# SSD scan and feed-forward: decay matrices as running products on VectorE, the scan in pairs of chunks, scores in four row tiles, weight conversion shared with ScalarE

## The chip, the cores and the metric

One core of one Trainium2 chip runs the kernel. The metric is device time in microseconds (us) of one execution; before the change it is 528.14 us, the median of 3 runs (527.07 to 530.32).

## The reference

A gated linear scan over 4 batches, 8 heads, 768 tokens, head dimension 32 and state size 16 (`x` is [4, 8, 768, 32], `a` [4, 8, 768], `B` and `C` [4, 8, 768, 16]), and then a feed-forward on the 3072 tokens of width 256:

```python
log_a = log(clip(a, 1e-6, 1))
# per chunk, state carried on:
cum = cumsum(la);  L = exp(cum_i - cum_j) where i >= j
y = (C B^T * L) x  +  (C state) * exp(cum)
state = exp(sum(la)) * state + sum_j B_j x_j exp(cum_last - cum_j)
# then, tokens x (head, dim) = 3072 x 256:
h = x @ w_in                     # 256 x 2048
out = (h * sigmoid(1.702 h)) @ w_out   # 2048 x 256
```

The weights arrive as float64 and are rounded to float32 on the chip. All else is float32.

## The kernel before

**Tiling.** The scan runs in chunks of 128 tokens, all 8 heads of a batch together: 24 chunks `n`, 6 per batch. Four chunks make a group of 512 tokens, 6 groups `g`. In a group the feed-forward is `hidden` (16 blocks `f` of 128 features, two 128x128 by 128x512 products each, SiLU on ScalarE, L329 to L335) and then `project` (4 blocks of 128 tokens, 16 products of 256 columns each, L337 to L345). A float32 product shows in the trace as two matmul instructions.

**One chunk of the scan.** `log_decay` (L226, GpSimd) writes log a above the diagonal, `decay` (L234) sums it with two 512-column products (`seg`, L239) and takes Exp on ScalarE (L242), and `causal` (L244, GpSimd) clears the other half: that is the decay matrix `L`, [j, head, i], 128x1024. `scale` (L250, GpSimd) decays B to the chunk's end and C from its start. `turn` (L261) transposes B, C and scaled C on TensorE and copies them out on VectorE. `scores` (L277) makes C.B for four heads at a time in two row tiles of 64 (`cb`, L284), and VectorE multiplies it into `L` (L285). `advance` (L288) makes the next state (`A` L296, VectorE L299 and L301). `finish` (L306) makes `y` from the old state (L315) and from `L` (L320, four column tiles of 32); VectorE copies it to `yT` (L326).

**Weights.** `narrow(i)` (L124 to L157) turns one of 16 pieces of 512 KB of float64 bits into float32: five instructions on VectorE and two on ScalarE. Pieces 0 to 7 are `w_in`, 8 to 15 `w_out`; a piece serves two blocks `f`. `fetch` (L111) loads a piece, five ahead.

**Order.** Every engine runs its instructions in the order in which they are written (`in_order`, L24). First come 8 steps (L349 to L363), each with a decay and a `narrow`; the first four also scan a chunk of group 0. Then, for each group (L365 to L396): 16 blocks of `hidden`, with the other 8 `narrow` in group 0 and, between the blocks, the scan of the next group's four chunks (one step of a chunk behind each block); then 4 blocks of `project`, each preceded by one decay matrix of the group after the next. All DMAs, loads and stores, are issued on SP's queue in written order (L101, L122, L162, L345). PSUM has two buffers each for `h` and `o` (`ff`), for `seg` and `cb` (`big`), and for the small tiles (`sm`).

Of the kernel before, what the change touches and what calls it, by code (L numbers as in the profile page):

```python
# [6 lines left out]
    make_identity,  # L7
    make_lower_triangular,
    make_upper_triangular,
)  # L10
# [9 lines left out]
P = 128  # L20
TG = 512


def in_order(tc):  # L24
    """Each engine runs its instructions in the order in which they are written."""
    last = {}
    for ins in list(tc.nc.cur_bb.bb.instructions):
        before = last.get(ins.engine)
        if before is not None:
            tc.add_manual_dep(  # L30
                ins, before.name,
                mybir.DependencyInfo(mybir.DependencyClass.NoSync,
                                     mybir.DependencyReason.DATA),
                reason="in_order")
        last[ins.engine] = ins
# [3 lines left out]
def kernel(  # L39
# [22 lines left out]
    nc = tc.nc  # L62

    # float64 weights, in two words an element
# [13 lines left out]
    assert NF // CG == 4 and NH * N == P and NH * D == DM and HB * D == P and HB * P == TG  # L78
# [6 lines left out]
    ps = ctx.enter_context(tc.tile_pool(name="ps", bufs=2, space=bass.MemoryType.PSUM))  # L85

    # ---- loads
    a_sb = const.tile([BH, S], FP32, name="a_sb")
# [4 lines left out]
    def load(g):  # L93
        rx[g] = raw.tile([P, CG, NH, D], FP32, tag="x", name=f"x{g}")
        rb[g] = raw.tile([P, CG, NH, N], FP32, tag="b", name=f"b{g}")
        rc[g] = raw.tile([P, CG, NH, N], FP32, tag="c", name=f"c{g}")
        for k in range(CG):
            b, c = divmod(g * CG + k, NC)
            sl = slice(c * P, (c + 1) * P)
            for dst, src in ((rb, B), (rc, C), (rx, x)):  # L100
                nc.sync.dma_start(out=dst[g][:, k], in_=src[b, :, sl, :].rearrange("h s d -> s h d"))  # L101

    # ---- weights: float64 bits, [low word, high word], to float32, a piece at a time
    PF = 2
    AHEAD = 5
# [18 lines left out]
    def narrow(i):  # L124
        """w = (-1)^sign x 2^(E - 1023) x (1 + high 2^-20 + low 2^-52), with the power of two
        0 below float32's normal range and infinite above it"""
# [4 lines left out]
        # an eighth of the mantissa: (1 + high 2^-23) - 7/8 is exact, the sum with low rounds  # L131
        u = wide.tile([P, PN], U32, tag="u", name=f"u{i}")
        nc.vector.tensor_scalar(out=u, in0=hi, scalar1=0x000FFFFF, scalar2=0x3F800000,
                                op0=ALU.bitwise_and, op1=ALU.bitwise_or)
        e = wide.tile([P, PN], U32, tag="e", name=f"e{i}")
        nc.vector.tensor_scalar(out=e, in0=hi, scalar1=0x7FF00000, scalar2=None,
                                op0=ALU.bitwise_and)
        m = wide.tile([P, PN], FP32, tag="m", name=f"m{i}")
        nc.scalar.activation(m, lo, AF.Copy, scale=2.0 ** -55)
        # the exponent field, moved to float32's place and bias; multiples of 2^20 are exact  # L140
        z = wide.tile([P, PN], FP32, tag="z", name=f"z{i}")
        nc.scalar.activation(z, e, AF.Relu, scale=8.0, bias=bias[:, 0:1])  # L142
        p2 = wide.tile([P, PN], U32, tag="p2", name=f"p2{i}")
        nc.vector.tensor_scalar(out=p2, in0=z, scalar1=float(255 << 23), scalar2=None,  # L144
                                op0=ALU.min)
        nc.vector.scalar_tensor_tensor(out=m, in0=u.bitcast(FP32), scalar=-0.875, in1=m,  # L146
# [5 lines left out]
        else:  # L152
            dst, split = w_out[:, f:f + PF, :], PF
        nc.vector.scalar_tensor_tensor(  # L154
            out=dst, in0=m.rearrange("p (k e) -> p k e", k=split), scalar=8.0,
            in1=p2.bitcast(FP32).rearrange("p (k e) -> p k e", k=split),
            op0=ALU.mult, op1=ALU.mult)  # L157

    bias = const.tile([P, 1], FP32, name="bias")
    nc.vector.memset(bias, -float(896 << 23))  # L160

    nc.sync.dma_start(out=a_sb, in_=a.rearrange("b h s -> (b h) s"))  # L162
    load(0)
    for i in range(AHEAD):
        fetch(i)

    # ---- constants
    ident = const.tile([P, P], FP32, name="ident")
    make_identity(nc, ident)
    upper = const.tile([P, P], FP32, name="upper")  # L170
    make_upper_triangular(nc, upper, 1.0, diag=True)
    lower = const.tile([P, P], FP32, name="lower")
    make_lower_triangular(nc, lower, 1.0, diag=False)
    ones = const.tile([P, P], FP32, name="ones")
    nc.vector.memset(ones, 1.0)
# [3 lines left out]
    nc.vector.memset(same, 1.0)  # L179
# [6 lines left out]
    # rows (head, state): one in the column head mod HB  # L186
    part = const.tile([P, HB], FP32, name="part")
    nc.vector.tensor_tensor(out=part, in0=same[:, 0:HB, 0], in1=same[:, HB:NH, 0], op=ALU.add)

    # ---- log a, and every decay that one token, or a whole chunk, has to itself  # L190
    a_ps = ps.tile([P, NC, BH], FP32, tag="sm", name="a_ps")
    for c in range(NC):
        nc.tensor.transpose(out=a_ps[:, c], in_=a_sb[:, c * P:(c + 1) * P],
                            identity=ident[0:BH, 0:BH])
    la = const.tile([P, NC, BH], FP32, name="la")
    nc.vector.tensor_scalar(out=la, in0=a_ps, scalar1=1e-6, scalar2=1.0,
                            op0=ALU.max, op1=ALU.min)
    nc.scalar.activation(la, la, AF.Ln)  # L198

    def summed(lhsT, name):  # L200
        t = ps.tile([P, NC, BH], FP32, tag="sm", name=name)
        nc.tensor.matmul(out=t, lhsT=lhsT, rhs=la, start=True, stop=True)
        return t

    to_end = const.tile([P, NC, BH], FP32, name="to_end")
    nc.scalar.activation(to_end, summed(lower, "end_ps"), AF.Exp)
    from_start = const.tile([P, NC, BH], FP32, name="from_start")
    nc.scalar.activation(from_start, summed(upper, "start_ps"), AF.Exp)
    whole_h = const.tile([P, NC * NB, NH], FP32, name="whole_h")
    nc.vector.tensor_tensor(  # L210
        out=whole_h, in0=summed(ones, "whole_ps").rearrange("p c (b h) -> p (c b) h", h=NH),
        in1=same[:, :, 0].unsqueeze(1).to_broadcast([P, NC * NB, NH]), op=ALU.mult)
    whole = const.tile([P, NC * NB], FP32, name="whole")
    nc.vector.tensor_reduce(out=whole, in_=whole_h, op=ALU.add, axis=AX.X)
    nc.scalar.activation(whole, whole, AF.Exp)

    # ---- the scan, a chunk at a time
    st = {}
# [3 lines left out]
    def heads(t, n):  # L222
        b, c = divmod(n, NC)
        return t[:, c, b * NH:(b + 1) * NH]

    def log_decay(n):  # L226
        """log a of token k where k <= i: [k, head, i]"""
        st[n] = {}
        st[n]["lu"] = lu = ssd.tile([P, NH, P], FP32, tag="lu", name=f"lu{n}")
        nc.gpsimd.tensor_tensor(  # L230
            out=lu, in0=upper.unsqueeze(1).to_broadcast([P, NH, P]),
            in1=heads(la, n).unsqueeze(2).to_broadcast([P, NH, P]), op=ALU.mult)

    def decay(n):  # L234
        """the decay from j to i, [j, head, i]; nothing for i < j yet"""
        lu = st[n].pop("lu")
        seg = ps.tile([P, 2, HB, P], FP32, tag="big", name=f"seg{n}")
        for t in range(2):
            nc.tensor.matmul(out=seg[:, t], lhsT=lower, rhs=lu[:, t * HB:(t + 1) * HB],  # L239
                             start=True, stop=True)  # L240
        st[n]["L"] = L = ssd.tile([P, NH, P], FP32, tag="L", name=f"L{n}", bufs=CG + 1)
        nc.scalar.activation(L, seg.rearrange("p t h i -> p (t h) i"), AF.Exp)  # L242

# [44 lines left out]
    def advance(n):  # L288
# [4 lines left out]
        if c == NC - 1:  # L293
            return
# [134 lines left out]
```

## Time and profile before

| | |
|---|---|
| runs | 530.32, 528.14, 527.07 us; median 528.14 |
| profiled execution | span 525.5 us from first to last instruction; its time with what lies around the span is not listed. The median is 2.6 us above the span |
| TensorE busy | 473.9 us (90%) |
| VectorE, ScalarE, GpSimd busy | 158.4, 116.9, 96.9 us |
| chain that ended last | TensorE 82%, VectorE 11%, ScalarE 2% |
| mean granted TensorE clock | 0.955 of full speed |

The profile is of one execution. A share of busy time is a mean over stages: here a stage of some 91 us before the first `h`, group 0 until 172 us, and then five groups that look alike.

### The profile page before, as it was taken

How to read it: one execution, taken by the hardware profiler on the slowest of the kernel's cores; microseconds unless marked ns; L12 is line 12 of the kernel's file. 1: busy time of each engine (PE TensorE's matmuls, PEld its weight loads, DVE VectorE, ACT ScalarE, POOL GpSimd, SP SyncE). 2: the span in 40 equal slices, each digit the busy share in tenths (PEclk: the TensorE clock that was granted, in tenths of full speed). 3: DMA queues.
4: the chain of work that ended last, by engine and by line, in shares of the span. 5: the costliest groups of instructions: out<-in, count | busy, mean ns of one | idle time of the engine just before them, and what ended most of it. 6: DMA issues, size and time to landing. Idle time of an engine off the chain costs nothing.

```text
span 525.5 us, 4898 instructions
## 1 busy us (share of the span) xinstructions
PE 473.9 (90%) x1932; PEld 284.7 (54%) x1932; DVE 158.4 (30%) x283; ACT 116.9 (22%) x167; POOL 96.9 (18%) x108
## 2 busy tenths in 40 slices
PE   4544476879999999999999999999999999999997
PEld 2222132333678444687444786445875446864586
DVE  1556567887600343000353001322002331000000
ACT  3111124434411122210323102223012221013200
POOL 6033344120222030231030312300321000000000
PEclk9677777989999999999999999999999999999999
DMA  8611254810000700000700002400000000000000
GB/s 118 249 40 41 50 71 131 153 37 1 1 20 11 90 0 2 1 20 19 82 0 1 10 11 46 54 1 1 11 20 11 0 0 1 22 20 0 1 20 20
DMA packets 82758, 18.23 MB, mean 35 GB/s; under 512 B 75536, under 2 KB 78608, under 8 KB 82736
## 3 DMA queue, kind: packets, MB, share of 16 engines
q1 hardware_dynamic: 82736, 17.93, 17.1%
q8 instruction: 15, 0.25, 0.2%
q14 instruction: 7, 0.06, 0.0%
HBM read 14.78 MB, written 3.15 MB: 34 GB/s over the span
## 4 chain that ended last, share of the span: by engine, by line
PE 82%; DVE 11%; ACT 2%; SPq 2%; issue 1%; DMA 1%; ACTq 0%; DVEq 0%
PE o L340 32%; PE h L332 29%; PE seg L239 7%; PE cb L284 5%; PE y L320 3%; DVE p L148 3%; PE y L315 3%; PE A L296 2%; DVE m L146 2%; ACT z L142 2%; SPq L101 2%; DVE p L144 1%; DVE w_in L154 1%; PE tp L266 1%; DMA bits<-in_moe_w_in_dram 1%
## 5 line engine op out<-in xcount | busy, mean ns | idle before, releaser
L332 PE MATMUL h<-yT,w_in 128*128 128x512 f32 x384 | 184.1, 610 | 0.0
L340 PE MATMUL o<-w_out,gT 128*128 128x256 f32 x768 | 168.8, 379 | 0.0
L340 PEld LDWEIGHTS o<-w_out,gT 128*128 128x128 f32 x768 | 145.8, 190 | 27.2 <-issue 8.3
L332 PEld LDWEIGHTS h<-yT,w_in 128*128 128x128 f32 x384 | 69.7, 193 | 76.7 <-issue 60.5
L335 ACT ACTIVATE gT<-h 128x512 f32<-128x512 f32 x96 | 57.3, 597 | 183.6 <-PE h L332 183.5
L343 DVE TENSOR_SCALAR ob<-o 128x256 f32<-128x256 f32 x24 | 10.2, 425 | 208.2 <-PE o L340 208.2
L246 POOL TENSOR_SCALAR_AFFINE_SELECT L<-L 128x1024 f32<-128x1024 f32 x24 | 27.5, 1146 | 232.0 <-ACT L L242 232.0
L242 ACT ACTIVATE L<-seg 128x1024 f32<-128x1024 f32 x24 | 24.6, 1023 | 144.4 <-PE seg L239 144.4
L239 PE MATMUL seg<-lu,lower 128*128 128x512 f32 x96 | 50.0, 647 | 3.2 <-POOL lu L230 3.2
L284 PE MATMUL cb<-CT,BT 64*128 64x512 f32 x96 | 30.9, 723 | 23.5 <-DVE CT L271 23.5
L230 POOL TENSOR_TENSOR lu<-upper,la 128x1024 f32<-128x1024 f32 x24 | 47.6, 1993 | 1.6 <-ACT la L198 1.6
L285 DVE TENSOR_TENSOR L<-L,cb 128x1024 f32<-128x1024 f32 x24 | 29.3, 1220 | 36.8 <-PE cb L284 36.8
L239 PEld LDWEIGHTS seg<-lu,lower 128*128 128x128 f32 x96 | 18.7, 205 | 21.5 <-issue 15.3
L284 PEld LDWEIGHTS cb<-CT,BT 64*128 64x128 f32 x96 | 8.2, 205 | 40.3 <-issue 15.3
L320 PE MATMUL y<-L,x 128*32 128x128 f32 x384 | 21.0, 301 | 3.1 <-DVE L L285 3.1
L315 PEld LDWEIGHTS y<-CsT,S 128*128 128x128 f32 x80 | 15.0, 208 | 13.0 <-issue 12.5
L326 DVE COPY yT<-y 128x256 f32<-128x256 f32 x24 | 10.2, 423 | 39.3 <-PE y L320 39.3
L257 POOL TENSOR_TENSOR Cs<-c,from_start 128x128 f32<-128x128 f32 x24 | 10.3, 430 | 56.7 <-PE tp L266 56.7
L266 PE MATMUL tp<-ident,Cs 128*128 128x128 f32 x24 | 6.8, 284 | 14.5 <-POOL Cs L257 14.5
L315 PE MATMUL y<-CsT,S 128*128 128x128 f32 x80 | 19.0, 323 | 0.0
L148 DVE SCALAR_TENSOR_TENSOR p<-bits,p 128x512 uint32<-128x512 uint32 x16 | 17.7, 1108 | 0.0
L144 DVE TENSOR_SCALAR p<-z 128x512 uint32<-128x512 f32 x16 | 9.1, 570 | 24.2 <-ACT z L142 24.2
(56 smaller groups left out, 204.1 us busy)
## 6 DMA issues: line engine op xcount, KB each, us to landing
bits<-in_moe_w_in_dram SPq DMA_DIRECT2D x8, 512.0 KB, 5.5
bits<-in_moe_w_out_dram SPq DMA_DIRECT2D x8, 512.0 KB, 3.5
x<-in_x_dram SPq DMA_DIRECT2D x24, 128.0 KB, 3.8
out_dram<-ob SPq DMA_DIRECT2D x24, 128.0 KB, 1.7
b<-in_B_dram SPq DMA_DIRECT2D x24, 64.0 KB, 3.7
c<-in_C_dram SPq DMA_DIRECT2D x24, 64.0 KB, 3.6
a_sb<-in_a_dram SPq DMA_DIRECT2D x1, 96.0 KB, 2.3
```

The source lines that it names most:

```text
L148: nc.vector.scalar_tensor_tensor(out=p2, in0=hi, scalar=0x80000000, in1=p2, op0=ALU.bitwise_and, op1=ALU.bitwise_or)
L230: nc.gpsimd.tensor_tensor(out=lu, in0=upper.unsqueeze(1).to_broadcast([P, NH, P]), in1=heads(la, n).unsqueeze(2).to_broadcast([P, NH, P]), ...
L239: nc.tensor.matmul(out=seg[:, t], lhsT=lower, rhs=lu[:, t * HB:(t + 1) * HB], start=True, stop=True)
L242: nc.scalar.activation(L, seg.rearrange("p t h i -> p (t h) i"), AF.Exp)
L246: nc.gpsimd.affine_select(out=L, in_=L, pattern=[[0, NH], [1, P]], compare_op=ALU.is_ge, fill=0.0, base=0, channel_multiplier=-1)
L284: nc.tensor.matmul(out=cb[:, t], lhsT=BT[r], rhs=CT[r], start=True, stop=True)
L285: nc.vector.tensor_tensor(out=L, in0=L, in1=cb.rearrange("p t h i -> p (t h) i"), op=ALU.mult)
L315: nc.tensor.matmul(out=y[:, t], lhsT=state[n - 1][:, t * HB:(t + 1) * HB], rhs=s["CsT"], start=True, stop=False, skip_group_check=True)
L320: nc.tensor.matmul(out=y[D * q:D * q + D, t], lhsT=rx[g][:, k, h], rhs=s["L"][:, h], start=(c == 0), stop=True, tile_position=(0, D * q), ...
L332: nc.tensor.matmul(out=h, lhsT=w_in[:, k, f * P:(f + 1) * P], rhs=yT[g][:, k], start=(k == 0), stop=(k == NK - 1))
L335: nc.scalar.activation(gT, h, AF.Silu, scale=GELU_SCALE)
L340: nc.tensor.matmul(out=o, lhsT=gT[f][:, k * P:(k + 1) * P], rhs=w_out[:, f], start=(f == 0), stop=(f == NF - 1))
```

## The change

- **Decay matrices.** `a` itself, broadcast to all 128 partitions, is loaded per chunk by a DMA (`spread`, 512 KB on arrival): for the first group from the input, with clipping on VectorE; later from a clipped copy with zeros at chunk starts, which the kernel writes to DRAM (`scratch`). One `tensor_tensor_scan` per chunk, 1024 elements, gives `L`: state = a x state + identity. `seg`, its Exp, `log_decay`, `causal` and `scale` are gone. `Be` takes its factor from the last column of `L`, on VectorE. The decay from the chunk's start comes from a scan per batch over rows of `a` (`decay_rows`), and is applied to C behind its transpose.
- **Pairs.** A step of the scan now takes two chunks (`p`, 12 pairs), two pairs per group. `scores` uses four row tiles of 32, each with its own PSUM bank (`cb`, one buffer of four banks).
- **Evacuation.** Copies of transposed B and C and of `y` move from VectorE to ScalarE.
- **Conversion.** In a piece the minimum moves to ScalarE: three instructions there (z, p2, m, one behind the other), five on VectorE. Fetches run four ahead instead of five.
- **Order.** Before the first `h` there are now 4 decays, 2 pairs and 3 pieces (before: 8 decays, 4 chunks, 8 pieces); 9 pieces and 4 decays lie between the blocks of `hidden` of group 0, 4 pieces, 4 decays and 2 pairs in its `project`, which runs over `f` outside and tokens inside. Pairs of later groups lie in `hidden`, decays in `project`.

```diff
+    def spread(n):
+        ra[n] = raw.tile([P, NH * P], FP32, tag="a", name=f"a{n}", bufs=4)
+        src = a[b, :, c * P:(c + 1) * P] if n < CG else scratch[b, c]
+        nc.sync.dma_start(out=ra[n]..., in_=src.unsqueeze(0).to_broadcast([P, NH, P]))
...
+    a_sb load; spread(0); load(0); spread(1); spread_rows(0); fetch(0); load(1)
+    spread(2); spread(3); fetch(1..3)
...
     def narrow(i):
+        nc.vector.tensor_scalar(out=e, in0=hi, 0x7FF00000, bitwise_and)
+        nc.scalar.activation(z, e, AF.Relu, scale=-8.0, bias=edge[:, 0:1])
+        nc.scalar.activation(p2, z, AF.Relu, scale=-1.0, bias=edge[:, 1:2])
+        nc.scalar.activation(m, lo, AF.Copy, scale=2.0 ** -52)
+        nc.vector.tensor_scalar(out=u, in0=hi, 0x000FFFFF, 0x41000000, and, or)
+        nc.vector.scalar_tensor_tensor(out=m, in0=u, scalar=-7.0, in1=m, add, add)
         nc.vector.scalar_tensor_tensor(out=p2, in0=hi, 0x80000000, in1=p2, and, or)
+        nc.vector.tensor_tensor(out=dst, in0=m, in1=p2, op=ALU.mult)
...
     def decay(n):
+        if n < CG:
+            nc.vector.tensor_scalar(out=t, in0=t, max 1e-6, min 1.0)
+            nc.vector.memset(first element of each head, 0.0)
+        nc.vector.tensor_tensor_scan(out=Ls[p][:, k], data0=t, data1=idents,
+                                     initial=0.0, op0=ALU.mult, op1=ALU.add)
+        if k == 1:
+            nc.vector.tensor_tensor(out=BE[p], in0=rb[p], in1=last column of Ls[p], mult)
...
+    def decay_rows(b):   # clip, memset, copy on GpSimd, then on VectorE:
+        nc.vector.tensor_tensor_scan(out=since[b], data0=t, data1=first, ...)
...
     def turn(p):
+        4 transposes (B, C of both chunks) into tp
+        nc.scalar.activation(s["BT"], tp[:, 0], AF.Copy)
+        for q in range(Q):   # 2
+            nc.scalar.activation(s["CT"][:, :, q], tp[:, 1], AF.Copy, scale=part[:, q:q + 1])
+        nc.vector.tensor_tensor(out=s["CsT"], in0=tp[:, 1], in1=since[b], op=ALU.mult)
...
     def scores(p):
+        cb = ps.tile([P, R, 2, Q * P], FP32, tag="cb", name=f"cb{p}", bufs=1)
+        for k in range(2):
+            for r in range(R):   # 4
+                nc.tensor.matmul(out=cb[:, r, k], lhsT=BT[rows, k], rhs=CT[rows, k],
+                                 tile_position=(32 * r, 0), ...)
+        nc.vector.tensor_tensor(out=Lv, in0=Lv, in1=cb, op=ALU.mult)   # 2048 elements
...
     def finish(p):   # all state products, then all products with L, then:
+        nc.scalar.activation(yT[g][...], y, AF.Copy)
...
+    def project_all(g, gT, between):   # group 0
+        for f in range(NF):
+            for do in between.get(f, []): do()
+            for k in range(CG):
+                nc.tensor.matmul(out=o[k // 2][:, k % 2], lhsT=gT[f][...], rhs=w_out[:, f], ...)
+        for k in range(CG): store(g, k, ...)
...
+    decay(0); decay(1); decay_rows(0); narrow(0)
+    for p in range(PG):   # 2
+        turn(p); advance(p); scores(p)
+        if p + 1 < PG: decay(2 * p + 2); decay(2 * p + 3)
+        narrow(1 + p); finish(p)
+    spread_rows(1); load(2); load(3); spread(4..7)
...
+    # hidden of group 0, after block f: narrow(3..7) at 0..4,
+    # decay(4..7) at 5, 7, 9, 11, narrow(8..11) at 6, 8, 10, 12
+    # project of group 0, before f: narrow(12..15) at 0, 2, 4, 6, decay(8..11) at 3, 7, 11, 15,
+    # pairs 2 and 3: turn, advance, scores, finish at 0, 1, 3, 6 and 8, 9, 11, 14; decay_rows(1) at 5
+    # hidden of groups 1 to 4: pairs at 0, 1, 2, 6 and 8, 9, 10, 14; project: one decay per block
```

## Rows read from the trace of the kernel before

**Rows 1.** Busy time in stretches of the span: us, engines, granted clock, DMA share, GB/s

```profile
0.00:91.00 91.00, 48.29 (x165) 22.07 (x166) 49.47 (x78) 21.36 (x30) 34.82 (x41) 0.77 0.43 100
91.00:172.10 81.10, 75.32 (x311) 45.27 (x310) 42.18 (x80) 27.73 (x40) 15.61 (x16) 0.96 0.18 37
172.10:247.90 75.80, 75.80 (x323) 46.30 (x323) 16.99 (x30) 14.94 (x21) 15.05 (x16) 1.00 0.15 21
467.30:525.50 58.20, 55.08 (x192) 36.11 (x191) 2.12 (x5) 9.55 (x16) 0.00 (x0) 1.00 0.03 12
```

**Rows 2.** Chain of waits in order of time: start us, us, what

```profile
222.02 1.72 PE seg L239 x4
...
439.46 27.82 PE o L340 x128
467.28 27.47 PE h L332 x64
```

**Rows 3.** Timeline of TensorE around one chunk: start us, us, engine, line, operation

```profile
171.93 1.88 PE L332 MATMUL h<-yT,w_in 128*128 128x512 f32 x4
...
173.65 0.27 PE L266 MATMUL tp<-ident,b 128*128 128x128 f32 x1
...
173.97 1.88 PE L332 MATMUL h<-yT,w_in 128*128 128x512 f32 x4
...
175.78 1.13 PE L284 MATMUL cb<-CT,BT 64*128 64x512 f32 x4
...
176.84 1.98 PE L332 MATMUL h<-yT,w_in 128*128 128x512 f32 x4
...
180.81 0.38 PE L315 MATMUL y<-CsT,S 128*128 128x128 f32 x2
...
182.26 1.98 PE L332 MATMUL h<-yT,w_in 128*128 128x512 f32 x4
```

**Rows 4.** Timeline of VectorE over one piece of weights, first and last instruction

```profile
94.68 0.42 DVE L133 TENSOR_SCALAR u<-bits 128x512 uint32<-128x512 uint32 x1
95.02 0.42 DVE L136 TENSOR_SCALAR e<-bits 128x512 uint32<-128x512 uint32 x1
96.28 0.43 DVE L144 TENSOR_SCALAR p<-z 128x512 uint32<-128x512 f32 x1 [0.85 <-ACT z L142]
96.63 0.69 DVE L146 SCALAR_TENSOR_TENSOR m<-u,m 128x512 f32<-128x512 f32 x1
98.56 1.21 DVE L285 TENSOR_TENSOR L<-L,cb 128x1024 f32<-128x1024 f32 x1
```

**Rows 5.** Timeline of ScalarE beside it

```profile
95.53 0.72 ACT L142 ACTIVATE z<-e,bias 128x512 f32<-128x512 uint32 x1 [1.23 <-DVE e L136]
...
100.44 0.67 ACT L139 ACTIVATE m<-bits 128x512 f32<-128x512 uint32 x1
```

**Rows 6.** Groups by line, shapes kept apart: busy us, mean ns, idle before

```profile
L271 DVE TENSOR_TENSOR CT<-tp,part 128x512 f32<-128x512 f32 x24 | 16.3, 681 | 0.0
L299 DVE TENSOR_TENSOR S<-A,same 128x256 f32<-128x256 f32 x20 | 8.4, 422 | 13.6 <-PE A L296 13.6
L335 ACT ACTIVATE gT<-h 128x512 f32<-128x512 f32 x96 | 57.3, 597 | 183.6 <-PE h L332 183.5
```

**Rows 7.** DMA over the first 30 us, rate in 40 slices, and issues by line

```profile
GB/s 0 0 111 98 83 135 108 112 107 133 102 127 113 113 121 110 301 380 385 385 407 401 393 391 382 391 382 380 262 11 0 0 0 0 0 0 0 0 0 0
...
x<-in_x_dram SPq DMA_DIRECT2D x4, 128.0 KB, 3.7
```

**Rows 8.** Timeline of SP's queue: the second DMA it issues

```profile
1.25 0.41 SPq L101 DMA_DIRECT2D b<-in_B_dram  x1
```

**Rows 9.** Busy time in two short stretches of group 0, columns as in rows 1

```profile
97.00:103.00 6.00, 6.00 (x32) 2.95 (x31) 5.08 (x10) 2.48 (x4) 0.00 (x0) 1.00 1.01 228
...
115.00:120.00 5.00, 5.00 (x15) 2.21 (x11) 4.07 (x10) 0.60 (x1) 0.00 (x0) 0.77 0.00 0
```

More of the change, by code (lines that the diff above doesn't have):

```diff
@@ L153, in narrow @@
             dst, split = w_out[:, f:f + PF, :], PF
[L154 to L162, printed above, removed]
-    load(0)
-    for i in range(AHEAD):
+        nc.vector.tensor_tensor(
+            out=dst, in0=m.rearrange("p (k e) -> p k e", k=split),
+            in1=p2.bitcast(FP32).rearrange("p (k e) -> p k e", k=split), op=ALU.mult)
@@ L165 @@
+    nc.sync.dma_start(out=a_sb.rearrange("p c s -> p (c s)"), in_=a.rearrange("b h s -> (b h) s"))
+    spread(0)
+    load(0)
+    spread(1)
+    spread_rows(0)
+    fetch(0)
+    load(1)
+    spread(2)
+    spread(3)
+    for i in range(1, AHEAD):
         fetch(i)
+    edge = const.tile([P, 2], FP32, name="edge")
+    nc.vector.memset(edge[:, 0:1], float((896 + 255) << 23))
+    nc.vector.memset(edge[:, 1:2], float(255 << 23))
     ident = const.tile([P, P], FP32, name="ident")
     make_identity(nc, ident)
-    upper = const.tile([P, P], FP32, name="upper")
@@ L171 @@
[L171 to L175, printed above, removed]
+    idents = const.tile([P, NH, P], FP32, name="idents")
+    nc.gpsimd.tensor_copy(idents, ident.unsqueeze(1).to_broadcast([P, NH, P]))
     same = const.tile([P, NH, D], FP32, name="same")
-    nc.vector.memset(same, 1.0)
+    nc.gpsimd.memset(same, 1.0)
@@ L185 @@
         fill=0.0, base=N - 1, channel_multiplier=-1)
[L187 to L218, printed above, removed]
+    part = const.tile([P, Q], FP32, name="part")
+    nc.vector.tensor_reduce(
+        out=part, in_=same[:, :, 0].rearrange("p (r q) -> p q r", q=Q), op=ALU.add, axis=AX.X)
@@ L219 @@
+    Ls, BE, st = {}, {}, {}
     state = {}
     yT = {}
[L222 to L232, printed above, removed]
-    def decay(n):
[L236 to L242, printed above, removed]
@@ new lines @@
+    since = {}
+    def decay_rows(b):
+        t = raf.pop(b)
+        nc.gpsimd.tensor_scalar(out=t, in0=t, scalar1=1e-6, scalar2=1.0,
+                                op0=ALU.max, op1=ALU.min)
+        first = ssd.tile([P, NC, P], FP32, tag="first", name=f"first{b}", bufs=1)
+        nc.gpsimd.memset(first, 0.0)
+        nc.gpsimd.tensor_copy(first[:, :, 0:1], t[:, :, 0:1])
+        nc.gpsimd.memset(t[:, :, 0:1], 0.0)
+        since[b] = ssd.tile([P, NC, P], FP32, tag="since", name=f"since{b}")
+        nc.vector.tensor_tensor_scan(
+            out=since[b].rearrange("p c s -> p (c s)"), data0=t.rearrange("p c s -> p (c s)"),
+            data1=first.rearrange("p c s -> p (c s)"),
+            initial=0.0, op0=ALU.mult, op1=ALU.add)
@@ new lines, in scores @@
+    def scores(p):
+        s = st[p]
+        BT, CT, L = s.pop("BT"), s.pop("CT"), Ls[p]
+        cb = ps.tile([P, R, 2, Q * P], FP32, tag="cb", name=f"cb{p}", bufs=1)
+        for k in range(2):
+            for r in range(R):
+                rows = slice(32 * r, 32 * r + 32)
+                nc.tensor.matmul(out=cb[:, r, k], lhsT=BT[rows, k],
+                                 rhs=CT[rows, k].rearrange("p q i -> p (q i)"),
+                                 start=True, stop=True, tile_position=(32 * r, 0),
+                                 skip_group_check=True)
+        Lv = L.rearrange("p k (r e) -> p k r e", r=R)
+        nc.vector.tensor_tensor(out=Lv, in0=Lv, in1=cb.rearrange("p r k e -> p k r e"),
+                                op=ALU.mult)
@@ new lines, in advance @@
+    def advance(p):
+        b, c = divmod(2 * p, NC)
+        Be = BE.pop(p)
+        nk = 1 if c + 2 == NC else 2
+        A = ps.tile([P, 2, NH * D], FP32, tag="sm", name=f"A{p}")
+        for k in range(nk):
+            nc.tensor.matmul(out=A[:, k], lhsT=Be[:, k].rearrange("p h n -> p (h n)"),
+                             rhs=rx[p][:, k].rearrange("p h d -> p (h d)"),
+                             start=True, stop=True, skip_group_check=True)
+        new = ssd.tile([P, 2, NH * D], FP32, tag="S", name=f"S{p}", bufs=3)
+        nc.vector.tensor_tensor(
+            out=new[:, :nk], in0=A[:, :nk],
+            in1=same.rearrange("p h d -> p (h d)").unsqueeze(1).to_broadcast([P, nk, NH * D]),
+            op=ALU.mult)
+        for k in range(nk):
+            if c + k > 0:
+                old = new[:, 0] if k else state[p - 1][:, 1]
+                nc.vector.scalar_tensor_tensor(
+                    out=new[:, k], in0=old, scalar=since[b][:, c + k, P - 1:P],
+                    in1=new[:, k], op0=ALU.mult, op1=ALU.add)
+        state[p] = new
@@ new lines, in finish @@
+    def finish(p):
+        g, half = divmod(p, PG)
+        b, c = divmod(2 * p, NC)
+        s = st.pop(p)
+        L = Ls.pop(p)
+        if half == 0:
+            yT[g] = ffn.tile([P, NK, TG], FP32, tag="yT", name=f"yT{g}")
+        y = ps.tile([P, 2, NK, P], FP32, tag="sm", name=f"y{p}")
+        first = True
+        for k in range(2):
+            if c + k == 0:
+                continue
+            old = state[p][:, 0] if k else state[p - 1][:, 1]
+            for t in range(NK):
+                nc.tensor.matmul(
+                    out=y[:, k, t], lhsT=old[:, t * P:(t + 1) * P], rhs=s["CsT"][:, k],
+                    start=first, stop=False, skip_group_check=True)
+                first = False
+        for k in range(2):
+            for h in range(NH):
+                t, q = divmod(h, HB)
+                nc.tensor.matmul(
+                    out=y[D * q:D * q + D, k, t], lhsT=rx[p][:, k, h],
+                    rhs=L[:, k, h * P:(h + 1) * P],
+                    start=False, stop=True, tile_position=(0, D * q), skip_group_check=True)
+        state.pop(p - 1, None)
+        nc.scalar.activation(
+            yT[g][:, :, 2 * half * P:2 * (half + 1) * P].rearrange("p t (k i) -> p t k i", k=2),
+            y.rearrange("p k t i -> p t k i"), AF.Copy)
@@ L365 @@
-    for g in range(NG):
-        nxt = [(g + 1) * CG + k for k in range(CG)] if g + 1 < NG else []
-        far = [(g + 2) * CG + k for k in range(CG)] if g + 2 < NG else []
-        if far:
-            load(g + 2)
+        store(g, k, o)
+    def project_all(g, gT, between):
+        o = [ps.tile([P, 2, DM], FP32, tag="ff", name=f"o{g}_{j}") for j in range(CG // 2)]
+        for f in range(NF):
+            for do in between.get(f, []):
+                do()
+            for k in range(CG):
+                nc.tensor.matmul(out=o[k // 2][:, k % 2], lhsT=gT[f][:, k * P:(k + 1) * P],
+                                 rhs=w_out[:, f], start=(f == 0 and k % 2 == 0),
+                                 stop=(f == NF - 1), skip_group_check=True)
+        for k in range(CG):
+            store(g, k, o[k // 2][:, k % 2])
@@ new lines @@
+    nc.vector.tensor_scalar(out=a_sb, in0=a_sb, scalar1=1e-6, scalar2=1.0,
+                            op0=ALU.max, op1=ALU.min)
+    nc.vector.memset(a_sb[:, :, 0:1], 0.0)
+    for b in range(NB):
+        nc.sync.dma_start(out=scratch[b].rearrange("c h s -> h c s"),
+                          in_=a_sb[b * NH:(b + 1) * NH])
+    decay(0)
+    decay(1)
+    decay_rows(0)
+    narrow(0)
+    for p in range(PG):
+        turn(p)
+        advance(p)
+        scores(p)
+        if p + 1 < PG:
+            decay(2 * p + 2)
+            decay(2 * p + 3)
+        narrow(1 + p)
+        finish(p)
@@ new lines, with at, scan_at @@
+    spread_rows(1)
+    for p in range(PG, 2 * PG):
+        load(p)
+    for n in range(CG, 2 * CG):
+        spread(n)
+    def at(places, i, *work):
+        places.setdefault(i, []).extend(work)
+    def scan_at(places, p, where):
+        for do, i in zip((turn, advance, scores, finish), where):
+            at(places, i, lambda do=do: do(p))
+    in_hidden = [{} for _ in range(NG)]
+    in_project = [{} for _ in range(NG)]
+    done = 1 + PG
+    for i in range(done, NF // PF):
+        at(in_hidden[0], i - done, lambda i=i: narrow(i))
@@ L370 @@
+    for g in range(NG):
+        if g + 2 < NG:
+            for j in range(PG):
+                load((g + 2) * PG + j)
+            for b in range(NB):
+                if (g + 2) * CG <= b * NC < (g + 3) * CG:
+                    spread_rows(b)
         gT = []
@@ L373 @@
             hidden(g, gT[f], f)
-            if g == 0 and f % PF == PF - 1:
-                narrow(NF // PF + f // PF)
-            k, step = divmod(f, NF // CG)
-            if not nxt:
-                continue
-            if step == 0:
-                scale(nxt[k])
-                turn(nxt[k])
-            elif step == 1:
-                scores(nxt[k])
-            elif step == 2:
-                advance(nxt[k])
-            else:
-                finish(nxt[k])
-        if far:
-            log_decay(far[0])
-        for k in range(CG):
-            if far:
-                decay(far[k])
-                if k + 1 < CG:
-                    log_decay(far[k + 1])
-                causal(far[k])
+            for do in in_hidden[g].get(f, []):
+                do()
+        if g + 2 < NG:
+            for k in range(CG):
+                spread((g + 2) * CG + k)
+        if g == 0:
+            project_all(g, gT, in_project[g])
+            continue
+        for b in list(raf):
+            decay_rows(b)
+        for k in range(CG):
             project(g, gT, k)
+            for do in in_project[g].get(k, []):
+                do()
     in_order(tc)
```

206 lines of the change are left out of this document (88 added, 118 removed).

## The prediction, made before the changed kernel ran

> **What bounds the kernel now.** I read the stretches first [rows 1]. From 172 us on TensorE is busy for the whole of each stretch at granted clock 1.00, and VectorE for under a quarter of it: there the time is TensorE's own work, and only what leaves TensorE counts. In the first 91 us TensorE is busy for 48 us, at a mean granted clock of 0.77, and VectorE for 49 us: no engine is full, they wait for each other. The second view, the chain of waits, gives the pieces of the TensorE-bound part [rows 2]: one decay matrix costs it 1.72 us, 16 blocks of `hidden` alone 27.47 us (1.717 a block), a `project` alone 27.82 us. The third, TensorE's timeline around one chunk [rows 3], gives the price of a scan step: four blocks with a chunk between them take 182.26 - 171.93 = 10.33 us, less 4 x 1.717 leaves 3.46 us a chunk, of which transposes 0.32 (173.65 to 173.97), `cb` 1.06 (175.78 to 176.84) and `y` 1.45 (180.81 to 182.26). The fourth is one weight piece on VectorE, with ScalarE beside it [rows 4, 5].
>
> **The TensorE-bound part, groups 1 to 4.** Removed are the decay products: 4 x 1.72 = 6.9 us in each `project` that had them. A pair of chunks cost 2 x 3.46 = 6.92 us. Six transposes become four: -0.2. `cb`: two row tiles take 1.06 us for four instructions of 0.43 each (a decay product's four take 1.72 [rows 2]), so they run two at a time, 0.86, with 0.20 for the block itself. Now a pair has 16 instructions of half the columns, 0.215 each; four at a time that is 0.86 + 0.20 = 1.06 in place of 2.12. The bounds, since no row shows four row tiles: 1.06, and 3.64 if they run one by one; two at a time as in the row gives 1.92. I take 1.06, since both the row tiles of the row run together. `A` and `y` stay. A pair: 6.92 - 0.2 - 1.06 = 5.66 us. A group: 27.47 + 11.3 + 27.82 = 66.6 us, four groups 266.4 us; the stretch they replace is 467.3 - 172.1 = 295.2 us. The last 58.2 us [rows 1] stay.
>
> [...]
>
> What hides the rest here: the copies moved to ScalarE cost it 0.9 to 1.8 us a pair for `B` and `C` (three passes of 256 columns; one of 512 is 0.60 us [rows 6]) against a SiLU of 0.60 us in a block of 1.72 us; the scans, up to 2.4 us, stand in `project` blocks of 6.9 us in which VectorE had one store; the strips are issued a group ahead. If that cover were gone, a pair's copies would add at most 1.8 us each, 14 us over eight pairs.
>
> **Group 0 and the start.** Here VectorE sets the pace, because it runs in written order and nearly everything passes through it. So I add up its list, from the first strip to the last scores of group 1's scan.
>
> A piece: before, 94.68 to 98.56, 3.88 us [rows 4], of which the last three instructions are 98.56 - 96.63 = 1.93 and the path from `e` to ScalarE's `z` 0.51 [rows 4, 5]. Now ScalarE has three instructions in a row, 0.72 + 0.72 + 0.67 = 2.1 us [rows 5], and VectorE's third waits for the last of them: 0.51 + 2.1 + 1.93 = 4.5 us; started back to back they overlap by some 0.1 each, so 4.4 (bounds 4.2 and 4.6). Sharing the work thus makes an undisturbed piece longer: VectorE does not use the time it is given, for the next piece's `e` stands behind this piece's product. 16 pieces: 70.4 us.
>
> A scan of 1024 elements: no row shows one. The nearest is the multiplication of two such inputs, 1.21 us [rows 4], the lower bound. The scan multiplies and adds, and each element needs the one before; two passes are 2.4 us. I take 2.4, the upper end, for that dependence. 12 scans and the two over rows of 768 (1.8 each): 12 x 2.4 + 3.6 = 32.4 us; at 1.21 it would be 16.3 us. [...]
>
> The rest: four clips, each two 512-element steps of 0.34 (94.68 to 95.02 [rows 4]) and a small memset, 0.8 x 4 = 3.2; six `Be` of 0.42 [rows 6], 2.5; four pairs, each 0.42 (`CsT`) + 0.68 (the masked state, 512 elements, as L271) + 0.9 (two state updates) + 2.4 (scores into `L`, twice 1.21) [rows 4, 6] = 4.4, 17.6 us. The list: 70.4 + 32.4 + 3.2 + 2.5 + 17.6 = 126.1 us.
>
> Waits on top. The first strip is the second DMA on SP, so it is issued at 1.25 us [rows 8] and lands 3.7 us later [rows 7]: 5.0. The second strip stands behind the first pair's six loads, 512 KB at some 110 GB/s, 4.7 us, and takes 1.7 itself (bounds 1.3 at 390 GB/s and 4.7 at 110 [rows 7]; its 512 B rows lie nearer to the 2 KB rows of the weights than to the 64 and 128 B of the loads); less the 3.2 of the first decay, 3.2. Piece 3's ScalarE work is written behind SiLU of block 0, which waits for `y` of pair 1 (2 x 1.45 us, twice that at half clock), its copy 0.6, the block 1.7 to 3.4 and SiLU 0.6: up to 9.5 us behind the scores, of which piece 2 covers 4.4: 5.0. So the list ends at 126.1 + 13.2 = 139.3 us, and its last scan and `Be` (2.8) lie behind the scores: these are done at 136.5. Then TensorE has `y` (2.9), two blocks of `project` (3.4), and VectorE two stores, 0.9, before PSUM is free, with 0.3 for hand-overs: group 1 starts at 144.0 us, where before it was 172.1.
>
> **Sum.** 144.0 + 266.4 + 58.2 = 468.6 us of span, 525.5 before: -28.1 before group 1 and -28.8 after. With the 2.6 us between span and median: 471 us.
>
> **Rivals.** (1) The scan goes at the rate of the row: 16 us less before group 1, 455 us. For it: inputs and output are those of a product at that rate; against: the dependence. 0.12. (2) Row tiles run one by one: 2.58 us a pair more, 8 pairs, 21 us: 492 us. For it: nothing; against: two tiles overlap in the row. 0.08. [...] 0.08. [...] (4) Strips arrive at the slowest rate of the loads, 4.7 us: 3 us more on each of the four first strips, 483 us, and up to 500 if slower still: 0.09. (5) Slower than before: 128 partitions read the same 4 KB of DRAM, which no row shows. SP's queue holds, ahead of the last strip of the start, 12 strips, 6 pairs of loads (28 us), 16 pieces (1.34 each, 21.5 us) and the rows, 52 us in all without the strips. It decides from 12.6 us a strip (42 GB/s): 52 + 151 + 3 = 206 us for the start of group 1, 62 us later than forecast. At 14 us a strip it gives some 550 us. Against: the slowest 0.75 us slices of the loads move 83 to 98 GB/s, in far smaller pieces [rows 7]. 0.03. That the change does not do what it says is in part the forecast: the conversion shared with ScalarE saves nothing; and were nothing gained before 172 us, the TensorE part alone would still give 499 us.
>
> **How the numbers follow.** The forecast has 0.60, with its own range 458 to 484 (a piece 0.2 either way, 3 us; the wait of 5 us absent; row tiles two at a time, +7; mode changes, -6). The range 449 to 491 takes in rivals 1 and 3 and most of 4, and leaves out 2, 5 and tails. Within 1%, 5.3 us, a measurement of this kernel would not be told from no change. Faster by more 0.95, within 0.02, slower 0.03.
>
> **What would show it.** The first `h` at about 48 us; group 1 from 144; groups of 66.6 us at clock 1.00; scans of 2.4 us; pieces 4.4 us apart where nothing lies between them; `cb` 1.06 us on TensorE's path. Wrong it is if scans or strips cost other than taken, if ScalarE's written order holds VectorE for longer than 5 us at the start, or if TensorE has gaps behind 144 us.

## The result, and the profile after

The changed kernel takes 462.8 us (median of 4 runs, 461.41 to 465.84), 0.877 of the time before (95% interval 0.873 to 0.881). The forecast was 471 us, range 449 to 491. The profiled execution has a span of 460.5 us.

The stretches of the changed kernel, cut at its own stages (the first `h`; the last block of `hidden` of group 0, 2.2 us ahead of the first product of its `project`; groups 1 to 4, of which one is shown; the end), with the columns of rows 1:

```profile
0.00:49.00 49.00, 16.64 (x125) 10.78 (x125) 29.63 (x42) 10.26 (x19) 8.27 (x15) 1.00 0.69 165
49.00:104.50 55.50, 35.91 (x61) 13.52 (x61) 34.08 (x52) 26.07 (x43) 2.45 (x4) 0.78 0.69 177
104.50:146.50 42.00, 38.38 (x255) 31.24 (x255) 30.96 (x41) 11.94 (x22) 0.00 (x0) 1.00 0.06 24
146.50:210.75 64.25, 64.25 (x319) 43.52 (x320) 18.76 (x19) 12.76 (x24) 3.81 (x4) 1.00 0.31 70
...
402.32:460.50 58.18, 55.09 (x192) 36.17 (x191) 2.12 (x5) 9.55 (x16) 0.00 (x0) 1.00 0.04 12
```

Group 1 begins at 146.5 us where it began at 172.1, 25.6 us earlier. Groups 1 to 4 take 402.3 - 146.5 = 255.8 us where they took 295.2, 39.4 us less, and TensorE is busy throughout them, as before. The last 58 us are as in [rows 1].

The chain of waits inside group 1 (start us, us, what) answers to [rows 2, 3]:

```profile
150.61 0.86 PE A L303 x4
151.47 1.72 PE h L353 x4
153.19 1.08 PE cb L288 x16
154.26 7.06 PE h L353 x16
161.33 0.89 PE y L333 x8
162.22 1.01 PE y L340 x32
163.23 3.63 PE h L353 x8
...
183.12 27.63 PE o L367 x128
```

No decay product is left; `project` is one run of 27.63 us. Scores of two chunks take 1.08 us where one chunk took 1.06, and `y` of two chunks 1.90 us (161.33 to 163.23). One chunk's `y` took 1.35 us in the same view of the kernel before (its 1.45 in [rows 3] are read from a timeline, in which neighbouring rows overlap):

```profile
180.98 0.22 PE y L315 x2
...
182.33 1.91 PE h L332 x4
```

VectorE's timeline over one weight piece in `hidden` of group 0, with its wait in brackets, answers to [rows 4]:

```profile
55.50 0.42 DVE L139 TENSOR_SCALAR e<-bits 128x512 uint32<-128x512 uint32 x1
55.84 0.42 DVE L147 TENSOR_SCALAR u<-bits 128x512 uint32<-128x512 uint32 x1
58.07 0.69 DVE L149 SCALAR_TENSOR_TENSOR m<-u,m 128x512 f32<-128x512 f32 x1 [1.81 <-ACT m L145]
...
60.01 0.42 DVE L139 TENSOR_SCALAR e<-bits 128x512 uint32<-128x512 uint32 x1
```

A piece takes 60.01 - 55.50 = 4.51 us, of which VectorE stands 1.81 us in front of the third instruction. Over the 16 pieces that is the first row of VectorE's waits (us in total, times, longest); the other two rows were not forecast:

```profile
DVE m L149 <- ACT m L145: 30.0, 16, 2.4
...
DVE since L256 <- POOL af L254: 4.3, 1, 4.3
DVE e L139 <- DMA bits<-in_moe_w_in_dram: 4.2, 1, 4.2
```

Behind `hidden` of group 0 it is TensorE that is nearly full. The stretch from the first product of `project` to group 1, with the columns of rows 1, and the last of the chain in it:

```profile
106.71:146.50 39.79, 36.16 (x249) 30.04 (x247) 28.86 (x36) 11.31 (x21) 0.00 (x0) 1.00 0.01 3
```

```profile
130.28 1.13 PE A L303 x4
131.41 3.45 PE o L378 x16
134.86 1.08 PE cb L288 x16
135.94 5.38 PE o L378 x24
...
142.77 3.65 PE o L378 x16
146.50 1.96 PE h L353 x4
```

The scan itself, from the groups by line:

```profile
L233 DVE TENSOR_TENSOR_SCAN L<-a,idents 128x1024 f32<-128x1024 f32 x24 | 54.8, 2283 | 0.1
```

2.28 us, 1.88 times the 1.21 us of a product of the same size [rows 4].

### The profile page after: what moved, and what is told of

Same layout as the page of the kernel before. It is cut to its first block, busy times and chain, and to the rows that moved or that the text cites. A ratio compares the mean times of both kernels' runs of the same rounds, so it can differ in the third digit from the quotient of the medians.

```text
span 460.5 us, 4656 instructions
## 1 busy us (share of the span) xinstructions
PE 401.8 (87%) x1896; PEld 264.6 (57%) x1896; DVE 167.7 (36%) x209; ACT 108.8 (24%) x194; POOL 18.3 (4%) x26
## 4 chain that ended last, share of the span: by engine, by line
PE 73%; DVE 12%; ACT 7%; DMA 3%; SPq 2%; issue 1%; POOL 1%; ACTq 0%
PE h L353 32%; PE o L367 30%; DVE L L233 3%; PE o L378 3%; PE cb L288 3%; ACT z L143 2%; ACT p L144 2%; PE y L340 2%; PE A L303 2%; SPq L104 2%; ACT m L145 2%; DMA af<-in_a_dram 2%; DVE m L149 2%; PE y L333 1%; DVE L L293 1%; DVE p L151 1%
## 5 line engine op out<-in xcount | busy, mean ns | idle before, releaser
L233 DVE TENSOR_TENSOR_SCAN L<-a,idents 128x1024 f32<-128x1024 f32 x24 | 54.8, 2283 | 0.1
L293 DVE TENSOR_TENSOR L<-L,cb 128x2048 f32<-128x2048 f32 x12 | 27.4, 2283 | 12.4 <-PE cb L288 12.4
L143 ACT ACTIVATE z<-e,edge 128x512 f32<-128x512 uint32 x16 | 11.5, 720 | 79.9 <-DVE e L139 75.9
L303 PE MATMUL A<-x,Be 128*128 128x256 f32 x40 | 12.8, 441 | 16.7 <-ACT yT L345 8.7
L288 PE MATMUL cb<-CT,BT 32*128 32x256 f32 x192 | 15.6, 445 | 7.3 <-ACT CT L274 7.3
L149 DVE SCALAR_TENSOR_TENSOR m<-u,m 128x512 f32<-128x512 f32 x16 | 11.1, 693 | 30.0 <-ACT m L145 30.0
L303 PEld LDWEIGHTS A<-x,Be 128*128 128x128 f32 x40 | 8.4, 217 | 22.3 <-ACT yT L345 9.5
L249 POOL TENSOR_SCALAR af<-af 128x768 f32<-128x768 f32 x4 | 11.1, 2767 | 210.4 <-DMA af<-in_a_dram 210.4
L288 PEld LDWEIGHTS cb<-CT,BT 32*128 32x128 f32 x192 | 9.7, 207 | 16.0 <-ACT CT L274 8.1
L340 PEld LDWEIGHTS y<-L,x 128*32 128x32 f32 x384 | 10.3, 114 | 5.4 <-DVE L L293 4.2
```

The source lines that it names most:

```text
L143: nc.scalar.activation(z, e, AF.Relu, scale=-8.0, bias=edge[:, 0:1])
L233: nc.vector.tensor_tensor_scan(out=Ls[p][:, k], data0=t, data1=idents.rearrange("p h i -> p (h i)"), initial=0.0, op0=ALU.mult, op1=ALU.add)
L288: nc.tensor.matmul(out=cb[:, r, k], lhsT=BT[rows, k], rhs=CT[rows, k].rearrange("p q i -> p (q i)"), start=True, stop=True, tile_position= ...
L293: nc.vector.tensor_tensor(out=Lv, in0=Lv, in1=cb.rearrange("p r k e -> p k r e"), op=ALU.mult)
L303: nc.tensor.matmul(out=A[:, k], lhsT=Be[:, k].rearrange("p h n -> p (h n)"), rhs=rx[p][:, k].rearrange("p h d -> p (h d)"), start=True, st ...
L340: nc.tensor.matmul(out=y[D * q:D * q + D, k, t], lhsT=rx[p][:, k, h], rhs=L[:, k, h * P:(h + 1) * P], start=False, stop=True, tile_positio ...
```

## The experiments

All are edits of the changed kernel, whose span is 460.5 us with group 1 from 146.5 us. "Start" below is the first `h` of group 1. Times are medians of 4 runs; ratios are to the kernel before, with 95% intervals.

**1. The old conversion.** In `narrow`, the VectorE and two ScalarE instructions of the kernel before. There are six on VectorE (the timeline of a piece in the trace before has six; the section on that kernel counts five):

```diff
-        nc.scalar.activation(p2, z, AF.Relu, scale=-1.0, bias=edge[:, 1:2])
+        nc.vector.tensor_scalar(out=p2, in0=z, scalar1=float(255 << 23), op0=ALU.min)
... and m first on ScalarE, with the old constants
```

> The changed kernel with the old conversion: minimum back on VectorE, two ScalarE instructions, both independent of each other (one for the low words first). Theory (VectorE's written order sets group 0, and sharing the conversion gains nothing): a piece that stands alone gets shorter, from 4.5 to about 3.9 us, 16 x 0.6 = 10 us at most; group 1 starts 5 to 10 us before 146.5, span 450 to 456 us. Rival (VectorE's amount of work sets it, so that the sharing is a gain): VectorE's list grows by 16 x 0.35 = 5.6 us, group 1 starts about 5 us later, span about 466 us. Groups 1 to 4 as they are, 64 us each.

Measured: 454.4 us, 0.860 (0.857 to 0.863), span 453.0, start at 138.98. First instructions of two neighbouring pieces on VectorE:

```profile
53.91 0.42 DVE L135 TENSOR_SCALAR u<-bits 128x512 uint32<-128x512 uint32 x1
...
57.79 0.42 DVE L135 TENSOR_SCALAR u<-bits 128x512 uint32<-128x512 uint32 x1
```

3.88 us a piece, what [rows 4] gave before. VectorE has more work a piece and is done sooner. The shared conversion costs this kernel 7.5 us.

**2. Pieces written one ahead.** The same instructions in another order on VectorE and ScalarE; for that, `u` gets a second buffer, and `z` is written over `e`:

```diff
     def narrow(i):
+        if i == 0: head(0)
+        if i + 1 < len(PIECES): head(i + 1)   # e, z, p2, m, u of the next piece
+        tail(i)                               # the last three of this one
```

> The changed kernel with VectorE's first two instructions of a weight piece, and ScalarE's three, written one piece earlier; the same instructions, another order. Theory (VectorE stands 30 us in front of the third instruction of the pieces, waiting for ScalarE, and that wait is in the chain that sets the start of group 1): most of the 30 us go, pieces come 2.7 to 3 us apart in hidden of group 0, and group 1 starts 15 to 28 us earlier, at 118 to 131 us; span 432 to 445 us. Rival (ScalarE, the arrival of the weights or TensorE at half clock is as late as VectorE): under 8 us are gained, span over 452 us.

Measured: 456.4 us, 0.863 (0.861 to 0.866), span 454.0, start at 139.98: 6.5 us, far less than the theory's 15 to 28, and what the rival allowed. Pieces came 2.7 us apart where nothing stood between them (54.90 to 57.64 us); one waited 2.9 us for ScalarE, and then VectorE met this:

```profile
76.09 0.43 DVE L145 TENSOR_SCALAR e<-bits 128x512 uint32<-128x512 uint32 x1 [10.18 <-DMA bits<-in_moe_w_in_dram]
```

Piece 7 was not there. Its fetch was issued only at 71.74 us. On SP's queue the fetch of piece 6 had stood 14.0 us for a buffer, until VectorE was done with piece 1, and went out at 44.4 us; then came 29 other loads, the twelve of group 2 last, and issuing them took the queue until 71.7 us, almost without waiting (1.1 us). The start was late too: the first instruction of piece 1, now in front of the end of piece 0, waited 4.65 us for its fetch, and the first `h` came at 55.33 us, 6.3 us later than in the changed kernel. `hidden` of group 0 was 9.0 us shorter and its `project` 3.9 us.

**3. `y` in the old order.**

```diff
     # finish, pairs with c > 0
-    four state products, then sixteen products with L
+    for k, t: one state product, then the four products with L of these heads
```

> The changed kernel with the products of y in the old order: state product of one half of the heads, then the four products with L of that half, and so on, in the pairs that do not begin a batch (8 of 12; pairs 4, 5, 7, 8, 10, 11 of the six in groups 2 to 5 among them). Theory (y fell from 2.9 to 1.9 us a pair because TensorE changes its tiling mode less often): y takes 2.7 to 2.9 us again in these pairs, 6 x 0.9 = 5 us in groups 1 to 4, span 465 to 467 us. Rival (y is shorter for another reason, so that order does not matter): span 460 to 461 us.

Measured: 470.8 us, 0.891 (0.888 to 0.894), span 468.9. The chain over one such pair, from its first row to the next `h`:

```profile
163.68 0.22 PE y L341 x2
163.90 0.36 PE y L330 x8
164.25 0.42 PE y L341 x2
...
166.22 0.36 PE y L330 x8
166.58 3.63 PE h L360 x8
```

2.90 us where the changed kernel has 1.90 in the same view, for the same instructions. The six pairs give 6.05 us behind the start (320.05 against 314.0 us); 2.35 more came ahead of it. The tiling mode (the whole array for state products and `h`, column tiles of 32 for products with `L`) changes 8 times in place of 2; read as the price of these six changes, 1.00 / 6 = 0.17 us each, an estimate.

**4. The decay products back on TensorE.**

```diff
     def project(g, gT, k):
+        if 0 < g < NG - 2:
+            products()      # two matmuls of 512 columns, ident by idents, into a cb buffer
```

> The changed kernel with the decay products' load on TensorE put back: two products of 512 columns, on the identity and with a result that nobody reads, ahead of each block of project in groups 1 to 3, 12 times; no exponential, nothing on GpSimd. Theory (groups 1 to 4 are TensorE's own work, so what was taken off it there came out in full): 12 x 1.72 = 20.6 us longer, groups 1 to 3 71 us each, span 481 us. Rival (part of that was hidden, or the groups are now held by VectorE or ScalarE): under 12 us.

Measured: 484.4 us, 0.919 (0.914 to 0.923), span 482.2, start at 147.59. In the chain they stand where they stood before:

```profile
184.22 1.72 PE seg L368 x4
185.93 6.91 PE o L379 x32
```

482.2 - 147.59 = 334.6 us behind the start against 314.0: 20.6 us, 12 x 1.72 to the tenth. Nothing of that part was hidden.

**5. The start in another order.**

```diff
-    decay_rows(0); narrow(0)
+    narrow(0); decay_rows(0)
... and load(4), load(5) behind hidden of group 0 in SP's queue
```

> The changed kernel with two things moved: the row scan of batch 0 behind the first weight piece on VectorE, and the loads of group 2 from ahead of hidden of group 0 to behind it on SP's queue, so that the fetch of piece 7 no longer stands behind loads that wait for buffers. Theory (VectorE's list with its waits sets the start of group 1): the waits of 4.3 us for the rows and 4.2 us for piece 7 go, group 1 starts 6 to 8 us before 146.5, span 452 to 455 us. Rival (VectorE catches up behind these waits anyway, since TensorE or ScalarE is as late): under 3 us, span over 457 us.

Measured: 457.9 us, 0.867 (0.866 to 0.869), span 456.2, start at 142.20: 4.3 us, between the two. The wait for piece 7 went; at the start only 1.8 us came out (first `h` at 47.2 us for 49.0): piece 0 reached ScalarE 3.65 us earlier, at 18.73 us, and the row scan, 1.76 us, now stands behind it in the same list. So VectorE began piece 11, the last in `hidden`, 6.1 us earlier (95.29 us for 101.38). But 2.2 us of that went in TensorE's last block of `hidden` and the transposes behind it, which took 4.42 us at a granted clock of 0.50 where the changed kernel took 2.26 at 1.00:

```profile
98.36:102.78 4.42, 4.42 (x8) 2.25 (x9) 2.16 (x5) 1.04 (x3) 0.00 (x0) 0.50 1.09 132
```

TensorE had stood 3.47 us before it, and 3.46 us in the changed kernel; why the clock fell in one and not in the other is not shown.

**6. Both: pieces ahead, start in the other order.**

> The weight pieces written one ahead, as in the run before, together with the two moves of the start. Theory (what swallowed the gain of the pieces written ahead was the wait of 10.2 us for piece 7, which stood behind the loads in SP's queue; behind about 101 us TensorE itself is full): group 1 starts 9 to 13 us before the 140.0 of the pieces alone, at 127 to 131 us, span 441 to 445 us. Rival (the fetches are late for lack of bandwidth, so that the wait only moves): over 450 us.

Measured: 448.4 us, 0.850 (0.848 to 0.851), span 446.7, start at 132.66: 7.3 us before experiment 2, short of 9 to 13. A wait for piece 1 at the start ate the rest, where writing ahead has nothing to hide behind; in experiment 2 it was 4.65 us, here it is longer:

```profile
28.27 0.43 DVE L145 TENSOR_SCALAR e<-bits 128x512 uint32<-128x512 uint32 x1 [9.59 <-DMA bits<-in_moe_w_in_dram]
```

**7. The scan as a product.**

```diff
-        nc.vector.tensor_tensor_scan(out=Ls[p][:, k], data0=t, data1=idents, ...)
+        nc.vector.tensor_tensor(out=Ls[p][:, k], in0=t, in1=idents, op=ALU.mult)
```

> The changed kernel with each scan of 1024 elements replaced by one product of the same two inputs; the running product is left out. It prices the serial scan. [...] Rival (scans fill time in which VectorE would wait for ScalarE or TensorE): under 5 us, span over 455 us.

Measured: 455.7 us, 0.864 (0.860 to 0.867), span 454.5, start at 140.46.

```profile
L233 DVE TENSOR_TENSOR L<-a,idents 128x1024 f32<-128x1024 f32 x24 | 29.2, 1218 | 0.1
```

12 x 1.07 = 12.8 us less work on VectorE gave 6.0 us, more than the rival's 5 and less than half of the work: the scan is half hidden in group 0, wholly behind it (454.5 - 140.46 = 314.0 us behind the start, as in the changed kernel). The trace says which half: `project` of group 0 began 6.6 us earlier (100.11 us for 106.71), of 8.5 us on the eight scans ahead of it, and was itself no shorter (40.35 us for 39.79), with four scans in it.

**8. Row tile by row tile.** `for r: for k:` in place of `for k: for r:`.

> The changed kernel with the eight products of the scores written row tile by row tile, both chunks of a tile behind each other, where the changed kernel goes round the four tiles. Theory (the 1.08 us come from four row tiles running at once, which needs neighbours in different tiles): neighbours now share a tile, about two run at a time, 1.6 to 1.9 us a pair, 8 pairs in groups 1 to 4, 4 to 7 us, span 465 to 467 us. Rival (the engine looks far enough ahead, or the tiles are bound by their issue): 1.08 us as before, span 460 to 461 us.

Measured: 463.2 us, 0.878 (0.876 to 0.880), span 460.8, `cb` 1.10 us. The order does not matter, as the rival had it.

**9. One row tile for all.** `rows = slice(0, 32)` and tile position (0, 0) in every product of the scores.

> The changed kernel with all sixteen matmul instructions of a pair's scores on the first row tile alone; the heads of the other three tiles are left out of the scores. The order of the products did not matter, so this prices the tiles themselves. Theory (the 1.08 us come from four row tiles at work together): on one tile the sixteen run one by one, 16 x 0.215 = 3.4 us and more a pair, 8 pairs in groups 1 to 4, 19 us longer there, span about 480 us. Rival (an instruction of 256 columns on 32 rows is that short by itself, 0.065 us, whichever tile it runs on): 1.1 us, span 460 to 462 us.

Measured: 495.9 us, 0.939 (0.936 to 0.943), span 494.0.

```profile
162.72 3.65 PE cb L288 x16
```

16 x 0.215 + 0.20 = 3.64 was the bound for one by one. So four tiles at work together make the 1.08 us, whatever order they are written in. The price is 2.57 us a pair. Span and start: 494.0 - 156.03 = 338.0 us behind the start against 314.0, 24.0 us, of which 8 x 2.57 = 20.6; the start itself is 9.5 us late. The other 3.4 us are 2 x 1.70: behind two of the eight `cb`, at 166.37 and 326.90 us, the next four blocks take 8.76 us where they take 7.06 behind the other six. At the first of the two it is clock: the mean granted clock was 0.56 from 166.4 to 169.8 us, after 3.65 us in which TensorE was busy throughout, but on one row tile. For the second no row gives the clock.

**10. Pieces ahead from the third on.** Experiment 6, but `head(i)` stays in its own place for pieces 0, 1 and 2; from piece 3 on it stands in front of the tail of the piece before.

> As the run with pieces ahead and the moved start, but pieces are written ahead only from the third on, so that VectorE does not wait at the start for the second piece (9.6 us in that run). Theory (from about 92 us TensorE is full, and what comes ahead of it counts): the first h comes at about 48 us, group 1 starts at 123 to 129 us in place of 132.7, span 437 to 443 us. Rival (the fetches, not VectorE, then hold hidden of group 0): within 2 us of 446.7.

Measured: 441.8 us, 0.837 (0.834 to 0.840), span 439.1, start at 125.06. This beats both kernels, the changed one by 21 us. Its stretches up to the start:

```profile
0.00:40.00 40.00, 13.08 (x80) 8.22 (x84) 25.52 (x37) 7.75 (x14) 7.20 (x14) 0.93 0.73 179
40.00:90.00 50.00, 37.45 (x124) 16.08 (x117) 42.50 (x66) 31.95 (x52) 4.18 (x4) 0.92 0.76 185
90.00:125.00 35.00, 34.99 (x243) 29.29 (x242) 26.27 (x30) 8.79 (x17) 0.00 (x0) 1.00 0.22 71
```

VectorE is now busy for 42.5 of 50 us in the middle, and TensorE for all of `project` of group 0, at clock 1.00.

**11. The old conversion with the start in the other order.** Experiments 1 and 5 together.

> The old conversion in the changed kernel, with the two moves of the start. Theory (a piece of the old form is 0.6 us shorter, and the moves take away the waits for rows and fetch, both in the same list): the gains add, 139 - 4 = 133 to 136 us for the start of group 1, span 446 to 450 us. Rival (TensorE's project of group 0 already holds the end with the old conversion): under 2 us from 453.0.

Measured: 446.2 us, 0.845 (0.843 to 0.847), span 444.4, start at 130.33. More than the sum: by start 16.2 us, where the two gave 7.5 and 4.3 apart. Most of the 4.4 us can be read from the traces. In experiment 1 the wait for piece 7 had grown to 6.15 us, from 4.24 in the changed kernel; here it is gone, 1.9 us more than experiment 5 had to win. And the 2.2 us that experiment 5 lost to the clock are not lost here: the same block and transposes took 2.26 us at 1.00.

## Why the prediction was right

**Groups 1 to 4 are TensorE's own work: shown.** Forecast 66.6 us a group, measured 64.0. Experiment 4 gives the decay products' price back to the tenth of a microsecond. `project` came out at 27.63 for 27.82, four row tiles at 1.08 for 1.06, and experiment 9 gives the upper bound, 3.65 for 3.64. What was mis-sized are the changes of tiling mode, which the sum left in `y`. The forecast's own range has them at -6 us; no run shows that term. What the runs showed in its place is experiment 3's 1.00 us for six changes, 0.17 each by estimate; whether the cost is that of the change or lies in something else that the order changes, such as the weight loads, no run here separates. A pair has 4 changes where it had 12, by the order of the products in the two kernels: eight fewer, 1.3 us, of which the sum had counted 0.20 with `cb`: 5.66 - 1.1 = 4.5 us, against (64.0 - 27.47 - 27.63) / 2 = 4.45 measured. Over eight pairs the miss is 9.7 of the 10.6 us by which groups 1 to 4 were forecast too long (266.4 for 255.8); a start 2.5 us later than forecast took some of it back, and the forecast ended 8 us high.

**VectorE's written order sets group 0: shown as far as `project`, with waits other than forecast.** Start forecast 144.0, measured 146.5; last scores of group 1's scan 136.5 and 140.15. In `hidden` the pieces stand as far apart as VectorE's list with its waits puts them, and edits of that list (experiments 1, 2, 5 and 7) move the first product of `project`, to 102.2, 104.1, 102.8 and 100.1 us from 106.7. Behind it the path was another than forecast. TensorE is busy for 36.2 of the 39.8 us of `project`, and without a gap from 130.28 us to group 1; the last scores were done 1.5 us before TensorE came to the products that read them (141.69 us). So the forecast's last leg, scores, then `y`, two blocks and the stores, was not what the end waited for. In experiments 2, 6 and 10 this stretch took 35.9 us, TensorE's own work: of what is taken off VectorE inside it, at most some 4 us can come out. The forecast's sum had no term for TensorE's own work in this stage. The terms that held: scans at the upper end, 2.28 for 2.4; pieces 4.51 for 4.4; first strip at 5.2 us for 5.0; 4.0 us of wait for the second, for 3.2; first `h` at 49.0 for 48. Between the 768 and the 1024 elements of the two scans (1753 and 2283 ns) an element costs 2.07 ns, and between products of 256 and 1024 elements (424 ns, and 1218 in experiment 7) 1.03, half of it. The terms that failed cancel in part: of the 5.0 us in front of the first SiLU only 0.6 came (piece 3 took 5.07 us for 4.51), and 8.5 us did that were not in the list, 4.3 for the rows, behind a strip of rows that landed 8 us after its issue and a clip of 2.77 us on GpSimd, and 4.2 for piece 7. The start is right partly by that luck.

**The conversion shared with ScalarE saves nothing: right in sign, too kind in words.** Undone, it gives 7.5 us. The working had the reason: three ScalarE instructions in a row where there was one on the path, and VectorE standing still meanwhile.

**That VectorE's 126 us are the pace: only in part.** Experiments 2 and 7 took most of 30 us of waits, and 12.8 us of work, out of its list and got 6.5 and 6.0 us. Behind VectorE stand two other limits close by: SP's queue, in which a fetch stood behind one that waited for a buffer and behind 29 loads to be issued, and TensorE, which in `project` of group 0 has 36 us of its own and in experiment 10 is full from 90 us to the start of group 1. Experiments 6 and 10 took them in turn.

**Rivals.** The scan at the rate of a product: refuted (2.28 us). Row tiles one by one: refuted (experiments 8, 9). TensorE at a lower granted clock in `project` of group 0: not seen, 1.00 from 104.5 us on in the changed kernel; in `hidden` of group 0, where TensorE was busy for 35.9 of 55.5 us, the mean was 0.78. Strips slow: they landed 6.9 us after issue (median; 7.1 for the first four), but no wait for one was longer than the 4.0 us at the start, so neither that rival's slower side nor the 12.6 us a strip of the last rival arose.

## What to carry to other kernels

An engine that runs in written order loses its partner's latency each time it hands work over and waits for it (1.81 us in the piece shown, 30.0 us over the 16); before moving an operation to another engine, write the path through both, not the sum on one, and put the next item's first half ahead of this item's second half. Then ask for each stage which engine's own work is the next limit: in `project` of group 0 it was TensorE's, and no shorter list on VectorE could win more than the 4 us between the two. In a part bound by TensorE, count every product and every change of tiling mode: both came out in full here (20.6 us behind the start in experiment 4, 6.05 in experiment 3). When one wait is removed, look at once at what stands behind it on the DMA queue: two of the gains here were eaten there until the loads were moved.

## What the runs showed of the hardware that was not expected

- Sixteen matmul instructions of 256 columns on four row tiles take 1.08 us in either order (1.10 tile by tile), 3.65 us on one tile: neighbours need not lie in different tiles.
- `y` took 2.90 us with eight changes between whole-array and column-tile products and 1.90 with two (experiment 3 and the changed kernel): some 0.17 us a change, an estimate.
- TensorE's mean granted clock was 0.56 for 3.4 us behind a stretch of 3.65 us in which it never stood, with one of the four row tiles at work (experiment 9, 166.4 to 169.8 us); behind one more of the eight such stretches the next four blocks took as long, 8.76 us, and behind the other six 7.06. With four tiles at work in 1.08 us the mean was 1.00 in each of groups 1 to 4 (changed kernel).
- A DMA of 512 KB that reads the same 4 KB of DRAM for 128 partitions landed 6.9 us after its issue (median of 20), against 4.3 to 5.8 for weight pieces of that size.
